# H3 convolution and feed-forward layer on one core: a larger descriptor room for GpSimd, `ones` read with a step of zero, the D skip added by a transfer

## The chip, the core and the metric

The kernel runs on one core of one Trainium2 chip. The metric is the time of one execution on the device in microseconds (us), as the median of several runs. The engines are TensorE (PE in the profile, its weight loads PEld), VectorE (DVE), ScalarE (ACT), GpSimd (POOL), and SyncE (SP), which here only issues transfers; 16 DMA engines carry out the transfers.

## What is computed

The reference, cut to what matters (S = 2048 positions, D = 1024 channels, F = 3584 hidden columns, all float32):

```python
xn = layernorm(A_q)
k_shift = causal depthwise convolution of A_k with A_shift_k   # 4 taps
kv = k_shift * A_v
y  = irfft(rfft(kv, 2*S) * rfft(A_ssm_k, 2*S))[:S]             # long causal convolution, per channel
y  = y + kv * A_ssm_D                                          # the D skip
out = A_q + xn * y + silu(xn @ B_w1) @ B_w2
```

The D skip is the same as adding `A_ssm_D` to the filter's first element, and that is how the kernel does it.

## The kernel before, in words

Two jobs share the core. The **feed-forward** job is matmuls in float16 with each operand split into a high and a low part, three matmuls for one product (lines 849 to 851 for the first matrix, 975 to 977 for the second). Its first matrix runs in plain units and then in units of seven products over pairs of columns (`units`); the second in plain form over 16 row tiles and two halves (`feed_forward`), and at the very end in eight units of seven products P1 to P7 (`units2`). Silu results go out to memory (`ht`) and come back as `wo` tiles, 13 of them in rotation. The weights of the second matrix are split by ACT and DVE into `x` tiles; those for `units2` are made while the plain form is still running, since they take over its places one by one.

The **convolution** job is done in eight groups of 128 channels. For each group SP loads the filter into `kf`; the D values are added to its first row; ACT takes the filter's squares for a scale (`hi<-kf`); `kv` is made in `acc` (DVE); PE transposes and transforms (`px`, `ps`); DVE does most of the transform and the product on `spec` and `tmp`; PE transforms back into `py`; and DVE multiplies by the normalized input `xg` into **`yt`**. A group has four `yt` tiles, and each goes out in two transfers of 128 KB that GpSimd issues and that **add** to the output in memory (helper `G`, line 279; `gated`, line 1589). `yt` has two places; a place comes free when both transfers of its tile have landed. The feed-forward results go out by the same helper (`out<-v`, `out<-hf`, `out<-w`, 256 KB each). GpSimd does little else, and issues them strictly in its program order. Before any of this the input is copied to the output by 16 plain transfers (`out<-in_x`).

The order of all instructions is fixed when the program is built: a planner (`Order.run`) holds a queue for each stream of work and always takes the head that can start first by its own price list, less a bias. A `G` has the price 1.1 us on GpSimd, and its data counts as landed 4.0 us later or when the planned transfer queue has come to it. Rings of tiles (`Ring`) say `ready()` when the uses of a place have been emitted in program order, not when they have happened. What the engines wait for on the chip are semaphores that follow from that order.

GpSimd writes descriptors of its transfers into a reserved stretch of on-chip memory; its size is `dynamic_dma_scratch_size`, 1024 bytes per partition. `ones`, a 128 x 128 tile of 512 bytes per partition, is read by PE in the warm-up and in the small sums of the scales (`norm`); `dr` is a tile of 512 bytes per partition for one group's D values.

Of the kernel before, what the change touches and what calls it, by code (L numbers as in the profile page):

```python
# [11 lines left out]
F32 = mybir.dt.float32  # L12
# [6 lines left out]
ADD, SUB, MUL = ALU.add, ALU.subtract, ALU.mult  # L19

P = 128
# [218 lines left out]
def h3_ffn_kernel(ctx, tc, x, kp, vs, fs, shift, dskip, w1, w2, cfwd, cinv, out):  # L240
    nc = tc.nc
# [3 lines left out]
    flag = defaultdict(Token)  # L245
# [12 lines left out]
    def size(a):  # L258
        n = 1
        for s in a.shape[1:]:  # L260
            n *= s
        return n

    def V(f, o, ins, us=None, m=0.15):
        return Op("DVE", us or 1.03 * (size(o) / 960 + 0.075), 0.16, f, ins, [o], m)
# [7 lines left out]
    def L(o, i, m=0.3):  # L273
        n = size(o) * o.shape[0] * mybir.dt.size(o.dtype)
        return Op("SP", 0.4, 0.1, lambda: nc.sync.dma_start(o, i), [i], [o], m, n)

    def G(o, i, m=0.3):
        n = size(i) * i.shape[0] * mybir.dt.size(i.dtype)
        return Op("POOL", 1.1, 4.0, lambda: nc.gpsimd.dma_start(o, i, accum_op=ADD), [i], [o], m, n)  # L279

    def v_tt(o, a, b, op, **k):
        return V(lambda: nc.vector.tensor_tensor(o, a, b, op=op), o, [a, b], **k)  # L282

    def v_stt(o, a, s, b, op0, op1, **k):
        return V(lambda: nc.vector.scalar_tensor_tensor(o, a, s, b, op0=op0, op1=op1), o,  # L285
                 [a, b] + ([] if isinstance(s, float) else [s]), **k)
# [31 lines left out]
    cst = ctx.enter_context(tc.tile_pool(name="cst", bufs=1))  # L318
# [10 lines left out]
    for n, e in enumerate((14 - 64, 10 - 64, 8 - 64, 64 - 23, 64)):  # L329
        nc.vector.memset(powers[:, n:n + 1], 2.0 ** e)  # L330
    invc = cst.tile([P, 1], F32, name="invc")
    ones = cst.tile([P, P], F32, name="ones")
    nc.vector.memset(ones, 1.0)
    ident = cst.tile([P, P], F32, name="ident")
    make_identity(nc, ident)
    taps = cst.tile([P, NG, TAPS], F32, name="taps")
# [12 lines left out]
    hts = Ring(order, wp, "ht", 4)  # L349
# [690 lines left out]
    def evacuate2(u, one, c, made, seen):  # L1040
# [3 lines left out]
        def copied(src, tok, to):  # L1044
            yield hfs.ready
            o, otok = hfs.tile([P, W])
            yield a_act(o, src, AF.Copy, invc2[:, 0:1])
            tok.set()
            yield G(to, o)
            otok.set()  # L1050
# [17 lines left out]
        yield v_stt(d, c[0], invc2[:, 0:1], d, MUL, ADD)  # L1068
        seen["P7"].set()
        yield G(at(u, 1, 1), d)  # L1070
        dt.set()
        if last:
# [9 lines left out]
        yield v_stt(a, c[0], invc2[:, 0:1], a, MUL, ADD)  # L1082
        c[1].set()
        yield L(at(u, 1, 0), a) if last else G(at(u, 1, 0), a)
        at_.set()

# [155 lines left out]
    def convolution(floor):  # L1242
# [5 lines left out]
        def ring(name, bufs, pool=ra):  # L1248
            return Ring(order, pool, name, bufs)

        kin_r, kf_r, dr_r, acc_r, hi_r, lo_r = (ring(*a) for a in (
            ("kin", 1), ("kf", 1), ("dr", 1), ("acc", 1), ("hi", 2), ("lo", 2)))
        tmp_r, csc_r, css_r = ring("tmp", 1), ring("csc", 2), ring("css", 2)
        ctxs["w2n"] = ring("w2n", 2)
        px_r, ps_r, py_r = ring("px", 1, ps_c), ring("ps", 2, ps_c), ring("py", 1, ps_c)
# [3 lines left out]
        more = {}  # L1259
# [14 lines left out]
        def loads():  # L1274
            for g in range(NG):
                for q in range(4):
                    b, ts = q // 2, q % 2 * TQ
                    yield kin_r.ready
                    kin, tok = kin_r.tile([P, 2 * TQ + HALO, P])
                    kt, kv = kin[:, 0:TQ + HALO], kin[:, TQ + HALO:]  # L1280
                    kins[g, q] = kt, kv, tok
                    yield L(kt, kp[g, b][:, ts:ts + TQ + HALO])
                    yield L(kv, vs[g, b][:, ts:ts + TQ])
                    flag["kin", g, q].set()
                    if q == 0:
                        yield kf_r.ready
                        kfs[g] = kf, _ = kf_r.tile([P, T2, 2, P], uses=4)
                        yield dr_r.ready
                        dr, dtok = dr_r.tile([1, P])
                        yield L(kf, fs[g])  # L1290
                        yield L(dr, dskip[g:g + 1, :])
                        yield v_tt(kf[0:1, 0, 0, :], kf[0:1, 0, 0, :], dr, ADD)
                        dtok.set()
                        flag["kf", g].set()

        def gate():
# [270 lines left out]
        def stage1_inv():  # L1567
            for g in range(NG):
                for t in TO:
                    yield flag["ipart", g, t]  # L1570
                    (hi, htok), (lo, ltok) = ipart.pop((g, t))
                    yield lambda: py_r.ready() or spare()
                    py, tok = (py_r if py_r.ready() else ff).tile([P, 2, 2, P])
                    for i in range(2):
                        def mm():
                            o = py[:, :, i, :]
                            ci = civ[:, t + 4 * i]
                            for c in range(2):
                                cs = slice(c * P, (c + 1) * P)
                                zs = slice(c * 2 * P, (c + 1) * 2 * P)  # L1580
                                nc.tensor.matmul(o, ci[:, 0, cs], hi[:, i, zs], start=(c == 0), stop=False)
                                nc.tensor.matmul(o, ci[:, 0, cs], lo[:, i, zs], start=False, stop=False)
                                nc.tensor.matmul(o, ci[:, 1, cs], hi[:, i, zs], start=False, stop=(c == 1))
                        yield T(mm, py[:, :, i, :], [hi[:, i], lo[:, i]], 0.66, m=1.0)
                    htok.set()
                    ltok.set()
                    add(gated(g, t, py, tok), CB)

        def gated(g, t, py, tok):
            yield flag["xg", g, t]  # L1590
            xg, xtok = xgs.pop((g, t))
            yield more["yt"].ready
            yt, ytok = more["yt"].tile([P, 2, 2, P], uses=2)
            sc, stok = scs[g]
            flat = [q.rearrange("p b i w -> p (b i w)") for q in (yt, py, xg)]
            yield v_stt(flat[0], flat[1], sc[:, 5:6], flat[2], MUL, MUL)
            tok.set()
            xtok.set()
            if t == TO[-1]:
                stok.set()  # L1600
            yield flag["copied"]
            for b in range(2):
                yield G(out4[b][:, :, t, g * P:(g + 1) * P], yt[:, b])
                ytok.set()
                flag["conv out"].set()

        for gen, bias in ((loads(), 0.05), (gate(), 0.04), (signal_parts(), CB), (stage1(), 0.02),
                          (transforms(), 0.02), (squares_w2(), 0.0), (rest(floor), 0.0)):
            add(gen, bias, floor)

    def change():

        yield flag["x done"]
        yield flag["spilled"]
        yield nm.ready
        early.close()
        convolution(max(order.free["DVE"], order.free["ACT"]))
# [95 lines left out]
```

## Time and profile before

| | |
|---|---|
| time, median of 3 runs | 1318.86 us (1317.51 to 1322.24) |
| the profiled execution's own time | 1314.44 us |
| its span | 1312.6 us, 1.84 us less than its own time |
| PE busy | 1255.1 us (96%) |
| DVE busy | 1166.1 us (89%) |
| ACT busy | 769.4 us (59%) |
| POOL busy | 126.3 us (10%), 127 adding transfers among it |
| software queue (GpSimd's transfers) | 24.91 MB, 14.6% of 16 engines' span |

Busy PE time is nearly the span, so the rest of the span is where PE had nothing to do: the start, some gaps, and the end. "Idle before, releaser" in a row says what an engine had waited for; "issue" as a releaser means that the profile shows no semaphore that it waited for.

### The profile page before, as it was taken

To read this page: it belongs to the slowest core of one execution; us is meant where nothing else is said; L and a number is where in the kernel's file an instruction comes from. 1 tells how busy PE (TensorE), PEld (TensorE's weight loads), DVE (VectorE), ACT (ScalarE), POOL (GpSimd) and SP (SyncE) were. 2 spreads that over 40 slices of the span, in tenths; PEclk is the share of its full clock that TensorE was granted. 3 is DMA by queue.
4 is the path that set the end of the run, shared out by engine and by line. 5 is a ranking of instruction groups with operands and counts; after the bars stand their busy time and mean duration, and the time that the engine had idled before them with its cause. 6 is when DMAs were issued, how large, how long until landed. Compare 5 with 4: busy or idle time off the path is not lost.

```text
span 1312.6 us, 17986 instructions
## 1 busy us (share of the span) xinstructions
PE 1255.1 (96%) x6146; PEld 610.2 (46%) x6146; DVE 1166.1 (89%) x1701; ACT 769.4 (59%) x1379; POOL 126.3 (10%) x133
## 2 busy tenths in 40 slices
PE   7899999899999989999999999999999999799993
PEld 6444544344444544445444544544544444344451
DVE  8999998999999679998999699699979979987981
ACT  6867987789566858878623622643442453535331
POOL 0000000000000011002100210210120020113222
PEclk8999999999999989999999999999999999899997
DMA  8456898899898789979975575687576478767855
GB/s 321 161 172 211 283 315 287 281 312 334 300 319 274 236 232 307 316 221 276 340 225 146 120 194 145 133 264 209 141 149 193 128 155 235 198 134 142 180 106 73
DMA packets 226012, 287.76 MB, mean 219 GB/s; under 512 B 16504, under 2 KB 135296, under 8 KB 223488
## 3 DMA queue, kind: packets, MB, share of 16 engines
q1 hardware_dynamic: 199440, 261.70, 61.2%
q0 software_dynamic: 26480, 24.91, 14.6%
q8 instruction: 48, 0.79, 0.3%
q14 instruction: 44, 0.36, 0.1%
HBM read 196.37 MB, written 98.57 MB: 225 GB/s over the span
## 4 chain that ended last, share of the span: by engine, by line
PE 43%; DVE 34%; issue 11%; DMA 7%; ACT 3%; POOL 2%; SPq 0%; POOLq 0%; DVEq 0%; ACTq 0%
DVE spec L282 10%; PE ff L851 7%; PE ff L849 7%; PE ff L850 7%; PE ff L976 6%; PE ff L977 6%; PE ff L975 5%; DVE tmp L282 5%; DVE ht L285 3%; DVE acc L285 3%; DVE x L285 2%; DMA out<-yt 2%; POOL out L279 2%; DVE spec L285 2%; DVE wo L285 1%
## 5 line engine op out<-in xcount | busy, mean ns | idle before, releaser
L976 PE MATMUL ff<-x,wo 128*128 128x512 f16 x864 | 328.4, 380 | 3.3 <-DVE x L285 3.3
L975 PE MATMUL ff<-x,wo 128*128 128x512 f16 x864 | 328.4, 380 | 1.5 <-ACT w L293 0.8
L977 PE MATMUL ff<-x,wo 128*128 128x512 f16 x864 | 328.4, 380 | 0.0
L849 PE MATMUL ff<-x,wo 128*128 128x512 f16 (+1 forms) x808 | 304.5, 377 | 7.3 <-DVE hf L282 3.2
L850 PE MATMUL ff<-x,wo 128*128 128x512 f16 (+1 forms) x808 | 304.5, 377 | 2.1 <-DVE x L285 2.1
L851 PE MATMUL ff<-x,wo 128*128 128x512 f16 (+1 forms) x808 | 304.3, 377 | 1.5 <-DVE wo L285 1.5
L282 DVE TENSOR_TENSOR spec<-spec 128x512 f32<-128x512 f32 (+2 forms) x256 | 261.7, 1050 | 1.7
L279 POOL DMA_DIRECT2D out<-yt x64 | 70.9, 1107 | 791.8 <-DMA wo<-ws 430.0
L977 PEld LDWEIGHTS <-wo 128*128 128x128 f16 x864 | 84.7, 98 | 106.8 <-issue 5.7
L975 PEld LDWEIGHTS <-wo 128*128 128x128 f16 x864 | 85.6, 99 | 97.5 <-issue 1.1
L976 PEld LDWEIGHTS <-wo 128*128 128x128 f16 x864 | 84.7, 98 | 99.4 <-issue 3.2
L851 PEld LDWEIGHTS <-wo 128*128 128x128 f16 x808 | 79.4, 98 | 98.5 <-issue 4.1
L850 PEld LDWEIGHTS <-wo 128*128 128x128 f16 x808 | 79.4, 98 | 96.6 <-issue 11.1
L849 PEld LDWEIGHTS <-wo 128*128 128x128 f16 x808 | 80.7, 100 | 86.9 <-issue 1.1
L282 DVE TENSOR_TENSOR tmp<-spec 128x2048 f32<-128x2048 f32 (+1 forms) x48 | 92.5, 1932 | 0.9
L285 DVE SCALAR_TENSOR_TENSOR ht<-hf,wsc,ht 128x512 f16<-128x512 f32 x104 | 76.4, 744 | 6.6 <-ACT ht L293 6.5
L293 ACT ACTIVATE ht<-hf,wsc 128x512 f16<-128x512 f32 x104 | 74.6, 719 | 6.8 <-DVE hf L282 4.5
L285 DVE SCALAR_TENSOR_TENSOR acc<-kin,taps,acc 128x512 f32<-128x512 f32 x96 | 71.4, 743 | 2.5 <-ACT acc L293 2.4
L293 ACT ACTIVATE wo<-raw,wsc 128x512 f16<-128x512 f32 x84 | 59.3, 711 | 15.0 <-DVE raw L282 15.0
L279 POOL DMA_DIRECT2D out<-v x39 | 36.7, 940 | 308.1 <-ACT v L293 274.8
L293 ACT ACTIVATE spec<-spec 128x1024 bf16<-128x1024 f32 x32 | 33.7, 1055 | 55.3 <-DVE spec L282 55.2
L285 DVE SCALAR_TENSOR_TENSOR wo<-raw,wsc,wo 128x512 f16<-128x512 f32 x84 | 61.9, 742 | 3.4 <-ACT wo L293 3.2
(192 smaller groups left out, 1820.3 us busy)
## 6 DMA issues: line engine op xcount, KB each, us to landing
wo<-hs SPq DMA_DIRECT2D x160, 256.0 KB, 3.7
w2n<-in_w SPq DMA_DIRECT2D x91, 256.0 KB, 4.6
ws<-wo SPq DMA_DIRECT2D x84, 256.0 KB, 3.5
wo<-ws SPq DMA_DIRECT2D x84, 256.0 KB, 4.6
hs<-ht SPq DMA_DIRECT2D x80, 256.0 KB, 3.5
raw<-in_w SPq DMA_DIRECT2D x28, 512.0 KB, 5.5
kin<-in_kp SPq DMA_DIRECT2D x32, 448.0 KB, 3.5
out<-v POOLq DMA_DIRECT2D x39, 256.0 KB, 4.5
```

The source lines that it names most:

```text
L279: return Op("POOL", 1.1, 4.0, lambda: nc.gpsimd.dma_start(o, i, accum_op=ADD), [i], [o], m, n)
L282: return V(lambda: nc.vector.tensor_tensor(o, a, b, op=op), o, [a, b], **k)
L285: return V(lambda: nc.vector.scalar_tensor_tensor(o, a, s, b, op0=op0, op1=op1), o, [a, b] + ([] if isinstance(s, float) else [s]), **k)
L293: nc.scalar.activation(o, i, func, scale=scale, **kw)
L849: nc.tensor.matmul(o, w[:, 0, k], xf[:, :, k, 0], start=first and k == 0, stop=False, **kw)
L850: nc.tensor.matmul(o, w[:, 0, k], xf[:, :, k, 1], start=False, stop=False, **kw)
L851: nc.tensor.matmul(o, w[:, 1, k], xf[:, :, k, 0], start=False, stop=last and k == KH - 1, **kw)
L975: nc.tensor.matmul(po, hx[:, n, 0, :], wc[:, n, 0, :], start=first and n == 0, stop=False, **kw)
L976: nc.tensor.matmul(po, hx[:, n, 0, :], wc[:, n, 1, :], start=False, stop=False, **kw)
L977: nc.tensor.matmul(po, hx[:, n, 1, :], wc[:, n, 0, :], start=False, stop=last and n == 3, **kw)
```

## The change

Five edits. The descriptors' room is doubled, from 1024 to 2048 bytes per partition. `ones` shrinks to one column that is read 128 times with a step of zero. The tile `dr`, its load by SP and the DVE addition of the D values go; in their place GpSimd issues a transfer of 512 bytes that adds the D values to `kf` directly. `yt` may take a place of the ring `hts` (the silu results) once the first matrix is done, if its own two are not ready. And the planner's price of a `G` falls from 4.0 to 3.0 us after the issue.

```diff
     def G(o, i, m=0.3):
-        return Op("POOL", 1.1, 4.0, lambda: nc.gpsimd.dma_start(o, i, accum_op=ADD), [i], [o], m, n)
+        return Op("POOL", 1.1, 3.0, lambda: nc.gpsimd.dma_start(o, i, accum_op=ADD), [i], [o], m, n)
...
-    ones = cst.tile([P, P], F32, name="ones")
-    nc.vector.memset(ones, 1.0)
+    one = cst.tile([P, 1], F32, name="one")
+    nc.vector.memset(one, 1.0)
+    ones = one.to_broadcast([P, P])
...
-                        yield dr_r.ready
-                        dr, dtok = dr_r.tile([1, P])
                         yield L(kf, fs[g])
-                        yield L(dr, dskip[g:g + 1, :])
-                        yield v_tt(kf[0:1, 0, 0, :], kf[0:1, 0, 0, :], dr, ADD)
-                        dtok.set()
+                        yield G(kf[0:1, 0, 0, :], dskip[g:g + 1, :])
...
-            yield more["yt"].ready
-            yt, ytok = more["yt"].tile([P, 2, 2, P], uses=2)
+            r = more["yt"]
+            yield lambda: r.ready() or flag["gemm1"]() and hts.ready()
+            yt, ytok = (r if r.ready() else hts).tile([P, 2, 2, P], uses=2)
...
-    nc = bacc.Bacc("TRN2", target_bir_lowering=False, num_devices=1, dynamic_dma_scratch_size=1024)
+    nc = bacc.Bacc("TRN2", target_bir_lowering=False, num_devices=1, dynamic_dma_scratch_size=2048)
```

Since the planner sets the order, it moves too, from the first group's filter on. GpSimd at the end of the program, before: `yt0` and `yt1` are the two places of `yt`, `x2` is the two halves of one tile, and `hf`, `w` and `v` are results of the last unit of the feed-forward job.

```order
L279 DMA out_0<-hf0_11807 128x512
L279 DMA out_0<-yt0_11832 256x1x128 x2
L279 DMA out_0<-v0_11692 128x512
L279 DMA out_0<-yt1_11875 256x1x128 x2
L279 DMA out_0<-yt0_11912 256x1x128 x2
L279 DMA out_0<-yt1_11946 256x1x128 x2
L279 DMA out_0<-hf1_11954 128x512
L279 DMA out_0<-w_11955 128x512
L279 DMA out_0<-hf0_12002 128x512
```

GpSimd at the same place now:

```order
L279 DMA out_0<-yt0_11792 256x1x128 x2
L279 DMA out_0<-yt1_11830 256x1x128
L279 DMA out_0<-hf1_11834 128x512
L279 DMA out_0<-yt1_11830 256x1x128
L279 DMA out_0<-yt0_11868 256x1x128
L279 DMA out_0<-v0_11689 128x512
L279 DMA out_0<-yt0_11868 256x1x128
L279 DMA out_0<-yt1_11911 256x1x128 x2
L279 DMA out_0<-hf2_11940 128x512
L279 DMA out_0<-w_11941 128x512
L279 DMA out_0<-hf1_11986 128x512
```

Four tiles and the last three results stand there as before; the other results stand between the halves of tiles. On PE the last `py` product has 63 feed-forward matmuls behind it, where it had 42.

GpSimd at the fifth group's `yt` tiles, before (group five's filter needs nothing of GpSimd there):

```order
L279 DMA out_0<-v0_9103 128x512
L279 DMA out_0<-yt0_9176 256x1x128 x2
L279 DMA out_0<-yt1_9206 256x1x128 x2
L279 DMA out_0<-yt0_9260 256x1x128 x2
L279 DMA out_0<-yt1_9302 256x1x128 x2
L279 DMA out_0<-v1_9368 128x512
```

And now, where a filter's D values (`kf<-in_dskip`) are issued ahead of the tiles:

```order
L279 DMA kf_8924<-in_dskip 1x16x8
L279 DMA out_0<-v0_9005 128x512
L279 DMA out_0<-yt0_9116 256x1x128 x2
L279 DMA out_0<-yt1_9146 256x1x128 x2
L279 DMA out_0<-yt0_9200 256x1x128 x2
L279 DMA out_0<-yt1_9242 256x1x128 x2
L279 DMA out_0<-v1_9259 128x512
```

Two places of `yt` in turn, as before: all 32 tiles of the program take `yt0` and `yt1` in turn, and none takes a place of `hts`.

ACT at the first group's filter, before (`hi<-kf` are the squares, `wo` and `ht` are high parts of the feed-forward job, `ff2<-ff3` frees one of its accumulators):

```order
L293 ACTIVATE wo9_2464<-t1_2357,wsc_181 128x512
L293 ACTIVATE hi0_2470,css0_2346<-kf_2361 128x1024
L293 ACTIVATE ff2_2488<-ff3_2404 128x512
L293 ACTIVATE wo10_2493<-raw3_2139,wsc_181 128x512
L293 ACTIVATE hi1_2476,css0_2346<-kf_2361 128x1024
L293 ACTIVATE hf2_2452<-hf2_2452,wsc_181 128x512
```

And now:

```order
L293 ACTIVATE wo9_2459<-t1_2357,wsc_181 128x512
L293 ACTIVATE ht1_2398<-x4_958,wsc_181 128x4x128
L293 ACTIVATE ff2_2484<-ff3_2403 128x512
L293 ACTIVATE wo10_2491<-raw3_2139,wsc_181 128x512
L293 ACTIVATE ht2_2405<-x4_958,wsc_181 128x4x128
L293 ACTIVATE hf2_2451<-hf2_2451,wsc_181 128x512
L293 ACTIVATE ht3_2509<-hf1_2416,wsc_181 128x4x128
L293 ACTIVATE wo11_2514<-raw3_2139,wsc_181 128x512
L293 ACTIVATE hi0_2467,css0_2346<-kf_2361 128x1024
L293 ACTIVATE v1_2486<-ff2_2484 128x512
```

The squares have moved seven places back, behind feed-forward work.

## Rows read from the trace of the kernel before

**Rows 1.** The page, part 1: busy time and share of the span.
```profile
PE 1255.1 (96%) x6146; PEld 610.2 (46%) x6146; DVE 1166.1 (89%) x1701; ACT 769.4 (59%) x1379; POOL 126.3 (10%) x133
```

**Rows 2.** Busy time of each engine by stretch; last columns granted clock, DMA share, GB/s.
```profile
478.90:482.90 4.00, 0.45 (x3) 0.05 (x2) 0.85 (x2) 0.99 (x2) 0.68 (x1) 0.88 0.33 77
...
1126.90:1143.20 16.30, 9.06 (x41) 3.91 (x40) 16.27 (x23) 10.36 (x17) 2.02 (x3) 0.92 0.79 209
1139.00:1147.70 8.70, 6.77 (x20) 2.60 (x21) 8.28 (x14) 4.76 (x8) 0.12 (x1) 0.61 0.25 55
...
1295.80:1312.60 16.80, 0.00 (x0) 0.00 (x0) 0.66 (x1) 0.00 (x0) 4.87 (x5) 0.56 0.61 86
...
1303.00:1306.00 3.00, 0.00 (x0) 0.00 (x0) 0.00 (x0) 0.00 (x0) 1.51 (x3) 0.50 1.03 123
```

**Rows 3.** POOL in order of time, third convolution group: start, us, instruction [idle before <-releaser].
```profile
725.37 1.10 POOL L279 DMA_DIRECT2D out<-yt  x1 [7.66 <-DVE yt L285]
729.79 1.11 POOL L279 DMA_DIRECT2D out<-yt  x1 [3.32 <-issue]
...
754.07 1.10 POOL L279 DMA_DIRECT2D out<-yt  x1 [2.82 <-issue]
754.65 1.45 POOL L279 DMA_DIRECT2D out<-v  x1
```

**Rows 4.** Transfers: count, KB, median us to landing; adding transfers after 1265, min/median/max.
```profile
wo<-hs SPq DMA_DIRECT2D x160, 256.0 KB, 3.7
...
out<-yt POOLq DMA_DIRECT2D x64, 128.0 KB, 3.9
...
DMA to landing us min/median/max: 3.1/4.0/6.6
```

**Rows 5.** What DVE waited for from 715 to 1070: us in total, times, longest.
```profile
DVE yt L285 <- ACT xg L293: 12.5, 2, 6.3
DVE yt L285 <- PE ps L1391: 11.2, 4, 2.8
DVE yt L285 <- DMA out<-yt: 11.1, 2, 5.7
```

**Rows 6.** All engines in order of time, the end of the program.
```profile
1283.40 0.75 DVE L285 SCALAR_TENSOR_TENSOR yt<-py,csc,xg 128x512 f32<-128x512 f32 x1 [7.01 <-DMA out<-yt]
...
1296.49 0.34 SPq L275 DMA_DIRECT2D out<-v  x1
...
1305.57 1.22 POOL L279 DMA_DIRECT2D out<-hf  x1
...
1284.20 0.27 PE L1581 MATMUL py<-zh,civ 128*128 128x256 f16 x1 [2.12 <-DVE yt L285]
```

**Rows 7.** DVE and PE in order of time, in the first unit of `units2`.
```profile
1142.02 2.07 DVE L285 SCALAR_TENSOR_TENSOR x<-x,tau,x 128x512 f16<-128x512 f32 x3
...
1146.61 0.63 PE L976 MATMUL ff<-x,wo 128*128 128x512 f16 x1
1147.04 0.63 PE L977 MATMUL ff<-x,wo 128*128 128x512 f16 x1
...
1148.37 0.38 PE L976 MATMUL ff<-x,wo 128*128 128x512 f16 x1
1148.59 0.38 PE L977 MATMUL ff<-x,wo 128*128 128x512 f16 x1
```

**Rows 8.** DVE and ACT in order of time at the first and fourth filter.
```profile
215.75 0.28 DVE L282 TENSOR_TENSOR kf<-kf,dr 1x128 f32<-1x128 f32 x1 [1.35 <-DMA kf<-in_fs]
...
216.06 1.06 ACT L293 ACTIVATE hi<-kf 128x1024 bf16<-128x1024 f32 x1 [1.32 <-DMA ws<-wo]
...
618.69 0.27 DVE L282 TENSOR_TENSOR kf<-kf,dr 1x128 f32<-1x128 f32 x1
...
626.67 1.04 ACT L293 ACTIVATE hi<-kf 128x1024 bf16<-128x1024 f32 x1
```

**Rows 9.** PE in order of time at the start: the warm-up.
```profile
1.20 6.54 PE L1648 MATMUL ft<-ones 128*128 128x128 f32 x44 [1.20 <-DVE ones L333]
```

More of the change, by code (lines that the diff above doesn't have):

```diff
@@ L1249, in ring @@
             return Ring(order, pool, name, bufs)
-        kin_r, kf_r, dr_r, acc_r, hi_r, lo_r = (ring(*a) for a in (
-            ("kin", 1), ("kf", 1), ("dr", 1), ("acc", 1), ("hi", 2), ("lo", 2)))
+        kin_r, kf_r, acc_r, hi_r, lo_r = (ring(*a) for a in (
+            ("kin", 1), ("kf", 1), ("acc", 1), ("hi", 2), ("lo", 2)))
         tmp_r, csc_r, css_r = ring("tmp", 1), ring("csc", 2), ring("css", 2)
```

## The prediction

> **What bounds the kernel now.** I read the busy shares first. PE is busy for 1255.1 of 1312.6 us [rows 1], so a change that adds or removes no matmuls can only gain what PE loses in gaps, at a lower clock, and after its last matmul. Next I read the stretches. After 1295.8 us PE does nothing more, yet the span runs 16.8 us on with POOL at work [rows 2]; that is the largest loss that one cause may explain. From 1126.9 to 1143.2 PE is busy 9.06 of 16.30 us, while DVE is busy 16.27: here DVE is late. From 478.9 to 482.9 PE loses another 3.55 us.
>
> Then POOL in order of time, in a convolution group. The second `yt` transfer starts 4.42 us after the first, and POOL sat idle 3.32 us "for issue", with no semaphore to wait for. A result transfer behind a `yt` transfer, however, starts only 0.58 us after it [rows 3]. The median `yt` transfer lands 3.9 us after its issue [rows 4]. My reading: the room for descriptors holds one `yt` transfer and one result, and not two `yt` transfers, so each `yt` waits until the one before it has landed. The code gives the sizes behind this: a `yt` transfer consists of 256 rows of 512 bytes, a result of 128 rows of 2 KB. If one `yt` and one result fit in the old room, two of each fit in the new one.
>
> That slow pace holds the two `yt` places, and DVE stands before `yt`: in the four groups between 715 and 1070 us it waited 12.5 + 11.2 + 11.1 us ahead of `yt` [rows 5], some 8.7 us in a group. The releasers named there are various, since ACT and PE had long been done in some of them; the place was what came last.
>
> **The change, part by part.** I sum against the profiled execution, 1314.44 us with a span of 1312.6; it is 4.4 us below the median of the runs, and I carry the difference over to the median.
>
> *The end, -9.9 us.* Before, the last result transfer is issued at 1305.57 and the span ends 7.0 us later [rows 6]. It was ready long before: PE's last matmul ended at 1295.67. With room for three transfers or more the eight `yt` transfers of the last group go out as DVE makes them, and the order helps: the last `py` has 63 matmuls behind it instead of 42, at 0.22 us 13.6 us. Then nothing is queued when PE ends. What is left: SP's store of the last tile starts 0.8 us after PE's end (1296.49), lands 3.5 to 4.5 us later (a `wo` load of the same size 3.7, adding transfers 3.1 to 6.6 [rows 4]), and the closing takes some 1.8 us (7.0 less 5.2 of landing, which I put between the median and the longest of [rows 4]). That is 6.1 to 9.2 us, I take 7.0: 16.9 - 7.0 = 9.9, with ends at 7.7 and 10.8.
>
> *The last group's wait, -2.1 us.* DVE waited 7.01 us for a `yt` place, and PE 2.12 us for that DVE row [rows 6]. It goes with the pace; at worst nothing of it goes.
>
> *The gap before `units2`, -8.3 us.* The gap is 16.30 - 9.06 = 7.24 us. In its last part the granted clock over 8.7 us is 0.61, so part of this stretch is at 1.2 instead of 2.4 GHz: eleven matmuls follow at a pitch of 0.43 instead of 0.22 us [rows 2, 7], 2.3 us more. DVE has no idle time there [rows 2] while it makes the last weights of `units2`, from 1142.02 on [rows 7]; it is simply late, and its last idle time before was in the sixth group, ahead of the third and fourth `yt` (2.8 and up to 5.7 us [rows 5]). With the new room, the third `yt` can start when the first tile's two transfers have landed: issue some 1.2 us after DVE's row begins, 1.1 us for the second, 4.0 of landing, so 6.3 us; before it was 1.2 + 4.42 + 3.9 = 9.5. The fourth's place comes free some 3 us after the third's, with two more issues, where the old pace made it wait 5.7 to 6.3 us more [rows 5]. Of the 8.5 us of both waits I take 6, since ACT still has to normalize the fourth's input. So DVE leaves the sixth group 6 us earlier. Does the new order eat this? Between the last `yt` of that group and the last weights it holds 83 us of DVE work instead of 77.5 (its rows by the mean durations), 5.4 more, and PE passes 360 matmuls to the same point instead of 330, 6.5 us more. That is a wash, 1.1 us to the good. I take 6.0 of the 7.24 us, and the whole 2.3, since pieces that stay short should not cost clock. Ends: 0 and 9.5.
>
> In the groups before, PE has next to no gaps, so DVE's 6 us there buy nothing by themselves.
>
> *The gap at 479, no change.* PE waits there for a `yt` whose place is held by a transfer that waits for the last copies of the input. Their place on SP is the same. The later transfers now share the engines with it: 0 to 0.5 us worse.
>
> *The D skip, +1.0 us.* Eight DVE rows of 0.28 us go [rows 8]; DVE is not the bound in most places, so I count nothing. Eight POOL issues come, at 1.1 us each like `yt` [rows 3], each ahead of `yt` or result transfers that then wait behind it for the filter's load. POOL has over 7 us idle ahead of a group [rows 3]. The data lands 1.1 + 3.1 to 6.6 us after the filter, where DVE took 0.28. From the third group on the squares come 8 us or more after the filter (the tightest is the fourth: 618.69, then 626.67 [rows 8]), which covers it. In the first they follow at once (215.75, then 216.06 on ACT [rows 8]); the order has put them seven ACT rows back, at 0.7 us 4.9 us, about what the transfer takes. If ACT is held, its silu rows and high parts are queued behind, and PE waits for those. So 0 to 3 us for the first two groups, and I take 1.0, for the order covers most of it. The Trainium skill, "DMA: Bandwidth & Descriptors", section "Anatomy of one DMA — SWDGE (gpsimd) path", gives such a transfer a fixed cost of about 2.0 us plus its bytes over 436 GB/s; by that the estimate for 512 bytes is 2.0 us and this term would be nil. It gives 2.3 us for a `yt` transfer, where the row has 3.9, so the trace does not bear it out for adding transfers.
>
> *`ones` with a step of zero, 0.* The warm-up ends at 7.74 us [rows 9], and PE then waits for DVE anyway. *`yt` in places of `hts`: 0,* since no tile goes there: `ready()` looks at what has been emitted, and by then the own place always counts as free. *The lower price of a `G`* acts through the order alone, counted above.
>
> Sum: -9.9 - 2.1 - 8.3 + 1.0 = -19.3 us, 1314.4 to 1295.1 for a profiled execution, and 1318.9 to 1299.6 for the median.
>
> **The rivals.** *Only the end gains.* DVE's factors are late all the same, because the planner, believing in cheaper transfers, has put them 5.4 us further back, or another gap of that size opens where the order moved (between 205 and 260 us, say). For it: PE's gaps there come from where DVE's rows stand, and such an order is touchy. Against: the sum above. Time: -9.9 - 2.1 + 1.0 = -11.0, 1308 us.
>
> *The room does not set the pace.* If adding transfers to memory are taken one at a time, or the room that counts is another, the pace stays at 3.7 us. For it: the spacing is just the time to landing. Against: the 0.58 us behind a `yt`. Then the end gains only the earlier `py`, 21 matmuls at 0.22, 4.5 us, the factors cost 5.4, the D skip 1.0: 1321 us, no difference.
>
> *Slower: the bursts starve PE.* Close to the end, three transfers keep all 16 engines busy (1.03) at 123 GB/s [rows 2]. Eight `yt` transfers, 1 MB, now in one burst, would hold them 8.5 us, and PE's `wo` loads, one per 2.6 us, queue beside them. The Trainium skill, "DMA: Bandwidth & Descriptors", section "Issuing engines are not separate DMA queues", says that transfers of all engines interleave on the same 16; that share agrees, and it speaks against buying speed with more in flight. The price: if the lead of the loads is below 8.5 us, each burst stalls PE by some 3.5 us and costs 2.5 us of clock, six bursts 36 us, less the gain 1318.9 + 36 - 19 = 1336 us. Against: 13 places at 2.6 us allow a lead of 33 us, and a load lands in 3.7 us [rows 4].
>
> **How the numbers follow.** The forecast, 1299.6 us, has 0.62, with its terms' bounds from 1290 to 1306; only the end gains, 0.23; the room does not set the pace, 0.09; slower by the bursts or in another way 0.06. The predicted time is 1299.6. The range from 1290 to 1310 takes in the first rival. About 0.5%, 6.6 us, is what a measurement of this kernel can tell from no change; faster than 1312.3 are the first two cases, so 0.85; the third case is the same, 0.10 with some of the last; slower 0.05.
>
> **What would show it.** In the changed profile the two halves of a `yt` tile start about 1.1 us apart with no idle time for issue; DVE's wait ahead of the third and fourth `yt` of a group falls from 8.7 to some 3 us; PE's gap between 1120 and 1150 is below 2 us, with a granted clock of 1.00; the span ends 7 us after PE's last matmul. If halves are still 3.7 us apart, the room was not it. If the gap before `units2` is still there, the order ate the 6 us. If PE waits for `wo` loads, the bursts collide. A longer warm-up than 6.54 us, or ACT idle ahead of the squares of the first filter for more than 3 us, would make small terms wrong. The prediction is most at risk from gaps at places that the new order opens, which no row of before shows.

## The result, and the profile after

The changed kernel takes 1296.5 us (median of 4 runs, 1296.0 to 1297.6) where the kernel before, measured beside it, takes 1318.2 (1316.1 to 1322.2): a ratio of 0.983, with a 95% interval from 0.981 to 0.986. The forecast was 1299.6 us with a range from 1290 to 1310. The medians are 21.7 us apart, the two profiled executions 17.7 in their spans, since the kernel before was profiled in an execution quicker than its four timed ones.

| profiled execution | before | after | change |
|---|---|---|---|
| span, us | 1312.6 | 1294.9 | -17.7 |
| PE's last matmul ends at | 1295.7 | 1290.6 | -5.1 |
| tail behind it | 16.9 | 4.3 | -12.6 |
| PE busy | 1255.1 | 1256.0 | +0.9 |
| PE idle before its end | 40.6 | 34.6 | -6.0 |

Part 1 of the page of the changed kernel, to be held against [rows 1]:

```profile
PE 1256.0 (97%) x6146; PEld 611.8 (47%) x6146; DVE 1164.3 (90%) x1693; ACT 769.5 (59%) x1379; POOL 132.7 (10%) x141
```

No engine's work has changed by more than 2 us, except POOL's, which grew by 6.4; the time came out of waiting. Two thirds of it came out of the tail. POOL in order of time, in the third convolution group and in the last, after (columns as in [rows 3]):

```profile
722.70 2.25 POOL L279 DMA_DIRECT2D out<-yt  x2 [7.62 <-DVE yt L285]
725.77 1.08 POOL L279 DMA_DIRECT2D out<-yt  x1 [0.82 <-DVE yt L285]
727.39 1.11 POOL L279 DMA_DIRECT2D out<-yt  x1 [0.53 <-issue]
...
1278.87 2.21 POOL L279 DMA_DIRECT2D out<-yt  x2 [0.77 <-DVE yt L285]
...
1289.11 0.89 POOL L279 DMA_DIRECT2D out<-hf  x1 [1.90 <-ACT hf L293]
```

Both halves of the first tile stand in one row ("x2"), 2.2 us for the two, where [rows 3] had 4.42 us from one start to the next. Those of the tile behind it start 1.62 us apart. In the last group the `yt` tiles are out at 1281, and POOL waits for ACT's last results instead of being late with them. All of the program's idle time of POOL that the trace puts down to "issue" has fallen from 165.2 to 2.8 us. The end, in order of time (PE and SP):

```profile
1290.22 0.38 PE L978 MATMUL ff<-x,wo 128*128 128x512 f16 x1
...
1291.41 0.34 SPq L275 DMA_DIRECT2D out<-v  x1
```

SP's store is the last thing that leaves, 0.8 us behind PE, and 3.5 us later the span ends. In [rows 6] POOL's last transfer left 9.1 us after that store.

Now the places where the forecast wanted the rest. Windows of the changed kernel (columns as in [rows 2]: busy time of PE, PEld, DVE, ACT, POOL, then clock, DMA share, GB/s):

```profile
240.00:275.00 35.00, 28.55 (x121) 12.26 (x119) 31.31 (x54) 26.09 (x46) 0.00 (x0) 0.90 0.86 272
725.00:1075.00 350.00, 349.60 (x1735) 170.53 (x1734) 314.58 (x383) 151.53 (x277) 55.65 (x56) 1.00 0.70 172
1126.90:1143.20 16.30, 10.16 (x37) 3.80 (x35) 15.65 (x23) 6.62 (x11) 1.75 (x2) 0.77 0.63 157
```

The first two windows for the kernel before:

```profile
240.00:275.00 35.00, 31.36 (x142) 14.21 (x141) 33.07 (x61) 29.56 (x53) 0.00 (x0) 0.95 0.89 289
725.00:1075.00 350.00, 345.77 (x1711) 167.49 (x1710) 306.36 (x377) 151.86 (x276) 51.38 (x51) 1.00 0.66 166
```

In the four groups between 725 and 1075 us PE lost 4.2 us in small gaps and now loses 0.4. The gap before `units2` is still there: 6.1 us idle where [rows 2] has 7.2, and a lower clock than before. And between 240 and 275 us PE now loses 6.5 us, where it lost 3.6. PE's own rows at these two places, after:

```profile
248.83 0.58 PE L850 MATMUL ff<-x,wo 128*128 128x512 f16 x1 [3.17 <-DVE hf L282]
259.01 0.59 PE L850 MATMUL ff<-x,wo 128*128 128x512 f16 x1 [3.28 <-DVE hf L282]
...
1134.11 0.38 PE L977 MATMUL ff<-x,wo 128*128 128x512 f16 x1 [2.16 <-DVE x L285]
1136.98 0.59 PE L977 MATMUL ff<-x,wo 128*128 128x512 f16 x1 [2.06 <-DVE x L285]
```

What DVE waited for from 715 to 1070 us (total, times, longest), to be held against [rows 5]:

```profile
DVE spec L282 <- ACT spec L293: 14.5, 8, 3.8
DVE yt L285 <- ACT xg L293: 9.1, 8, 1.5
...
DVE yt L285 <- PE py L1580: 2.3, 4, 0.6
```

The wait ahead of `yt` has gone from 34.8 to 9.1 us, 8.7 to 2.3 in a group, as forecast (with the short waits for `py`, 1.5 us before, it is 36.3 to 11.4). But a wait that was not there has come up behind it: 14.5 us for ACT's `spec` rows. At the sixth group's last `yt` one sees how (DVE):

```profile
1051.79 0.75 DVE L285 SCALAR_TENSOR_TENSOR yt<-ff,csc,xg 128x512 f32<-128x512 f32 x1 [1.50 <-ACT xg L293]
1055.44 0.69 DVE L282 TENSOR_TENSOR spec<-spec,ps 128x512 f32<-128x512 f32 x1 [2.90 <-ACT spec L293]
```

and ACT in the same 4 us:

```profile
1052.13 1.05 ACT L293 ACTIVATE hi<-kf 128x1024 bf16<-128x1024 f32 x1
...
1053.17 1.05 ACT L293 ACTIVATE hi<-kf 128x1024 bf16<-128x1024 f32 x1
...
1054.21 0.71 ACT L293 ACTIVATE acc<-kin,taps 128x512 f32<-128x512 f32 x1
1054.83 1.07 ACT L293 ACTIVATE spec<-ps 128x512 f32<-128x512 f32 x2
```

DVE wants the copy of a product (`spec<-ps`), which stands on ACT behind the next filter's squares and a tap. As I read it, ACT had time for all of that while DVE stood before `yt` for 5 us, and now it hasn't. DVE's idle time from 725 to 1075 us has fallen by only 8.2 us (43.6 to 35.4), some 2.5 in a group of about 106 us, where the forecast took 6.0.

### The profile page after: what moved, and what is told of

Its sections match the earlier page's. It is cut to its first block, busy times and chain, and to the rows that moved or that the text cites. A ratio compares the mean times of both kernels' runs of the same rounds, so it can differ in the third digit from the quotient of the medians.

```text
span 1294.9 us, 17972 instructions
## 1 busy us (share of the span) xinstructions
PE 1256.0 (97%) x6146; PEld 611.8 (47%) x6146; DVE 1164.3 (90%) x1693; ACT 769.5 (59%) x1379; POOL 132.7 (10%) x141
## 4 chain that ended last, share of the span: by engine, by line
PE 69%; DVE 19%; DMA 6%; ACT 3%; issue 3%; SPq 0%; DVEq 0%; ACTq 0%
PE ff L977 11%; PE ff L978 11%; PE ff L976 11%; PE ff L850 9%; PE ff L852 9%; PE ff L851 9%; DVE spec L282 4%; DVE x L285 2%; DVE tmp L282 2%; DMA w2n<-in_w 2%; DVE ht L285 2%; PE ps L1386 2%; PE ps L1388 2%; PE ps L1387 2%; DVE wo L285 1%
## 5 line engine op out<-in xcount | busy, mean ns | idle before, releaser
L293 ACT ACTIVATE v<-ff,invc 128x512 f32<-128x512 f32 x40 | 27.4, 686 | 91.4 <-PE ff L978 76.6
```

Source lines behind the costliest of these rows:

```text
L293: nc.scalar.activation(o, i, func, scale=scale, **kw)
```

## The experiments

Each time stands beside runs of the kernel before on the same chip. Its medians lie 5 us apart (1313.2 to 1318.2), so ratios are compared. Where the last column says "one run" there is no interval.

| run | room | D skip | differs also in | us | ratio to before, 95% |
|---|---|---|---|---|---|
| changed kernel | 2048 | transfer | | 1296.5 | 0.983 (0.981 to 0.986) |
| e1_old_room | 1024 | transfer | | 1323.5 | 1.007 (1.005 to 1.010) |
| e2_price4 | 2048 | transfer | price 4.0 | 1296.3 | 0.986 (0.983 to 0.989) |
| e3_old_room_price4 | 1024 | transfer | price 4.0 | 1323.2 | 1.007 (1.006 to 1.009) |
| e4_room1536 | 1536 | transfer | | 1295.9 | 0.986 (0.984 to 0.988) |
| e5_dve_dskip | 1536 | DVE | | 1289.5 | 0.981 (0.979 to 0.983) |
| e6_no_dskip | 2048 | left out | | 1295.1 | 0.985 (0.983 to 0.988) |
| e8_full_ones | 1536 | transfer | full `ones` | 1294.9 | one run |
| e10_small_edits | 1024 | DVE | | 1315.6 | 1.000 (0.998 to 1.001) |
| e11_room1280 | 1280 | DVE | | 1290.9 | one run |
| e9_factors_first | 1536 | DVE | factors earlier | 1288.7 | 0.979 (0.976 to 0.982) |
| e12_factors_a_little | 1792 | DVE | factors a little earlier | 1284.7 | 0.976 (0.974 to 0.978) |
| e13_factors_room1792 | 1792 | DVE | factors earlier | 1286.8 | 0.978 (0.975 to 0.980) |

**The room undone, the rest kept.**

```diff
-    nc = bacc.Bacc("TRN2", ..., dynamic_dma_scratch_size=2048)
+    nc = bacc.Bacc("TRN2", ..., dynamic_dma_scratch_size=1024)
```

> The changed kernel with the old room (1024) and nothing else different: the instructions stand in the same order on every engine. Theory (the room sets the pace of the `yt` transfers): halves of a `yt` tile are 3.7 us apart again with some 2.5 us of idle time for issue between them, DVE waits for a `yt` place again in the last groups, PE ends at some 1294 us instead of 1290.6, and the tail after PE's last matmul is some 13 us (16.9 of the kernel before, less the 4 us by which the last `py` comes earlier). Time 1312 to 1322 us. Rival (the new order alone brings the gain, the room is only used when it is there): within 3 us of the changed kernel, 1294 to 1300.

1323.5 us, 2.2 to 2.4% above the changed kernel by the ratios and slower than the kernel before. POOL in its second-last group, in order of time:

```profile
1199.51 1.10 POOL L279 DMA_DIRECT2D out<-yt  x1 [2.48 <-issue]
1203.04 1.09 POOL L279 DMA_DIRECT2D out<-yt  x1 [2.42 <-issue]
1206.61 1.10 POOL L279 DMA_DIRECT2D out<-yt  x1 [2.48 <-issue]
```

3.5 us from one half to the next, with the idle time for issue back in each row, 153.0 us in all. The trace also has the landing of each transfer. In this run 53 `yt` transfers stand right behind another `yt` transfer; none starts before that one has landed, and 51 start 0.26 to 0.38 us after. In the kernel before it is the same (0.26 to 0.33 us). In the changed kernel 49 of the 53 start before the landing. The tail is 13.3 us, and PE ends at 1311.2 us, where I had expected some 1294: in this order the room is worth more through PE's waits than through the tail. The order of the rows is that of the changed kernel, so these 2.2 to 2.4% are the room's alone. That the rest of the change costs 0.7% was not expected; it is followed up below.

**The planner's price put back.**

```diff
-        return Op("POOL", 1.1, 3.0, ...
+        return Op("POOL", 1.1, 4.0, ...
```

> The changed kernel with the planner's old price of an adding transfer (4.0 instead of 3.0), the room kept at 2048: only the order differs. Theory (the room brings the gain, the order is worth a few us either way): 1295 to 1303 us; halves of a `yt` tile back to back; the last `py` again has some 42 matmuls behind it, so the tail after PE's last matmul grows from 4.3 to 6 to 9 us. If the gap before `units2` (6.1 us idle in 1125 to 1150) stands because the new order puts DVE's factors 5.4 us later, it shrinks here to 0 to 2 us and gives back 4 to 6 us. Rival (the order is what gained): 1308 to 1318.

> Old room and old price: the kernel before with the cheap `ones`, the D skip as a transfer and the free choice of a place for `yt`. Theory: 1318 to 1321 us, the D skip costing 0 to 3 us and the other two edits nothing; tail 16 to 18 us. Rival (the small edits carry part of the gain, DVE having eight rows less): 1312 to 1316.

With 3.0 and with 4.0 every row of every engine stands in the same place: the price edit has no effect, and the two runs repeat the changed kernel and the run before. They show how far equal programs differ: 0.983 and 0.986, 1.007 and 1.007. It also shows that the planner's shift of DVE's rows, which the prediction laid to cheaper transfers, is the D skip's. Both runs missed what I expected of the tail (the last `py` did not move back) and of the old room (10 us slower than before, not 0 to 3).

**How much room it takes.**

> The changed kernel with a room of 1536, half way. Theory: if the old room holds one `yt` transfer (256 rows) and one result (128 rows) but not two `yt` transfers, this room holds two `yt` transfers at least, and the halves of one tile go back to back, while the next tile waits when it comes within 4 us. Time 1296 to 1303 us, idle time for issue on POOL only behind pairs. Rival (a room must hold more for the next transfer to start, or the pace goes by another measure): halves 2.5 to 4 us apart, time 1308 to 1320.

> The same with a room of 1280. If room is counted in rows and 1024 holds one `yt` transfer of 256 rows and one result of 128 but not two `yt` transfers, 1024 holds 384 to 511 rows, and 1280 holds 480 to 639: two `yt` transfers fit in the upper part of that. If they fit, halves start 1.1 us apart and the time is 1288 to 1296 us; if not, 3.7 us apart and 1310 to 1318 us.

Half of the added room brings the whole gain, and in a single run a quarter brings nearly all of it (PE ends at 1281.0 us, but the tail is 8.1 us, where it is 4.9 with 1536). The second of these runs, and the one with 1536 beside it, have the D skip on DVE. POOL's idle time for issue falls on, though:

| room | 1024 | 1280 | 1536 | 1792 | 2048 |
|---|---|---|---|---|---|
| run | e10 | e11 | e5 | e12 | changed kernel |
| issue, us in all | 164.8 | 34.2 | 32.2 | 5.8 | 2.8 |

(The last two have other orders of rows; in the order of the changed kernel a room of 1536 has 28.4.) With 1280 two `yt` transfers fit, but the third still waits: in the last group transfers start 1.5 to 2.1 us apart. Whether the room is counted in rows or in bytes was not tried.

```profile
1274.04 1.10 POOL L279 DMA_DIRECT2D out<-yt  x1 [1.00 <-issue]
1275.64 1.10 POOL L279 DMA_DIRECT2D out<-yt  x1 [0.50 <-issue]
1277.49 1.11 POOL L279 DMA_DIRECT2D out<-yt  x1 [0.75 <-issue]
```

**The D skip back on DVE, in a room of 1536 and of 1024.** The first has the room and the two small edits (`ones`, the places of `hts`) in the order of the kernel before; the second has the small edits alone. Both keep the new price of a `G`, which moves no row here either.

```diff
-                        yield G(kf[0:1, 0, 0, :], dskip[g:g + 1, :])
+                        yield L(dr, dskip[g:g + 1, :])
+                        yield v_tt(kf[0:1, 0, 0, :], kf[0:1, 0, 0, :], dr, ADD)
+                        dtok.set()
```

> The changed kernel with the D skip back on DVE (its tile and its load from SP with it) and a room of 1536, which leaves the memory for that tile and was as good as 2048 in the run before. Every engine's rows then stand in the order of the kernel before (the warm-up's operand apart), so this is the room alone. Theory (the D skip's transfer costs some 10 us, since the old room with the small edits was 9.9 us slower than the kernel before): 1284 to 1291 us; one PE gap of some 3.2 us at 254 instead of two at 249 and 259, and less than 2 us of PE idle time from 1120 to 1150. Rival (the D skip costs about the 1.0 us of the prediction with the new room, and cost 10 only where POOL was blocked): 1294 to 1298 us.

> The run with the D skip on DVE, but in the old room of 1024: what is left of the change is the step of zero in `ones` and the free choice of a place for `yt`; every engine's order is that of the kernel before. Theory (these two cost and bring nothing, the room is all): within 4 us of the kernel before, halves of a `yt` tile 3.7 us or more apart, a tail of 16 to 18 us. Rival (one of the two edits is worth something): 5 us or more off the kernel before.

The small edits alone change nothing (1.000, 0.998 to 1.001). Room alone takes 1.9% off, more than the whole change does. This pair differs in nothing but the room, and every row stands in the same order, so one can compare stretches between the same two rows of PE: around 480 us, where the first `yt` tiles go out; from the third group to a matmul ahead of the gap before `units2`; and from there to one behind that gap. The small edits alone, in the old room:

```profile
462.82:515.33 52.51, 46.53 (x201) 20.81 (x200) 42.46 (x53) 32.91 (x68) 7.71 (x7) 0.90 0.91 254
...
725.15:1110.48 385.33, 380.49 (x1873) 183.18 (x1871) 341.24 (x417) 162.21 (x294) 55.35 (x55) 1.00 0.67 172
1110.48:1164.80 54.32, 47.91 (x210) 21.90 (x209) 52.34 (x78) 24.67 (x41) 6.92 (x8) 0.91 0.67 172
```

The same stretches with the room of 1536:

```profile
464.46:509.26 44.80, 42.06 (x201) 19.52 (x200) 40.23 (x51) 31.88 (x67) 7.71 (x7) 1.00 1.00 293
...
721.27:1099.30 378.03, 378.03 (x1872) 183.92 (x1870) 343.95 (x419) 163.89 (x295) 55.28 (x55) 1.00 0.69 176
1099.30:1151.65 52.35, 46.35 (x211) 21.38 (x210) 50.99 (x76) 24.56 (x41) 6.92 (x8) 0.93 0.69 174
```

In the groups PE takes 7.3 us less, 4.8 of them gaps. Around the gap before `units2` it takes 2.0 us less, but of its 6.4 us of idle time only 0.4 goes. The tail goes from 15.2 to 4.9 us. Around 480 us 7.7 us go; there the kernel before, in the old room too, takes 49.0 us for the same rows, so 3.5 us of this vary from one execution to the next. The last group gives 4.1 us.

I had expected less than 2 us of idle time before `units2`, so that expectation fell, and with it the prediction's own reserve, that a new order might eat DVE's time: no new order is at work here. Half of that idle time is one row, the same in both (PE in order of time, the old room first):

```profile
1140.42 1.12 PE L1356 MATMUL px<-ident,acc 128*128 128x128 f32 x4 [3.24 <-DVE ht L285]
...
1127.50 0.66 PE L1356 MATMUL px<-ident,acc 128*128 128x128 f32 x4 [3.24 <-DVE ht L285]
```

The kernel before has the same 3.24 us there. This is PE's wait for DVE's `ht` rows of the next convolution group, and the room did not change it.

**The D skip left out, the order kept.**

```diff
-                        yield G(kf[0:1, 0, 0, :], dskip[g:g + 1, :])
+                        op = G(kf[0:1, 0, 0, :], dskip[g:g + 1, :])
+                        op.emit = lambda: None
+                        yield op
```

> The changed kernel, its order untouched on every engine, with the eight D skip transfers not issued (the output lacks the D skip). Theory A (the cost lies in the order that the planner makes around a D skip that it believes to land late): nothing is gained, 1293 to 1298 us, the PE gaps at 249 and 259 stay. Theory B (the cost is the transfer itself, POOL's issue and the wait for its landing): 1284 to 1291 us, and the gaps at 249 and 259 shrink to one of 3 us.

1295.1 us and 0.985: the eight transfers cost nothing that can be measured. What costs is the order that the planner makes for a D skip that it takes to land late. PE's two gaps stay without any transfer (PE in order of time):

```profile
246.72 0.59 PE L850 MATMUL ff<-x,wo 128*128 128x512 f16 x1 [3.21 <-DVE hf L282]
257.16 0.58 PE L850 MATMUL ff<-x,wo 128*128 128x512 f16 x1 [3.28 <-DVE hf L282]
```

With the D skip on DVE (the run with 1536) there is one:

```profile
254.18 0.38 PE L850 MATMUL ff<-x,wo 128*128 128x512 f16 x1 [3.24 <-DVE hf L282]
```

In the old room the same order and its transfers cost 0.7%. One wait there looks like the transfer's own: the second half of a `yt` tile stands on POOL beside a D skip, and the profile names the filter's load as its releaser (POOL in order of time, changed kernel in the old room, and the landing of the first of these transfers):

```profile
606.01 1.09 POOL L279 DMA_DIRECT2D out<-yt  x1 [6.38 <-DVE x L285]
615.64 1.10 POOL L279 DMA_DIRECT2D out<-yt  x1 [8.54 <-DMA kf<-in_fs]
616.22 1.36 POOL L279 DMA_DIRECT2D kf<-in_dskip  x1
...
DMA to landing us min/median/max: 9.3/9.3/9.3
```

But the first half landed 9.3 us after its start, at 615.3, and the second starts 0.31 us later, as the others do in this room. So this wait is the room's too. What makes up the 0.7% was not found.

**The full `ones`.**

> The changed kernel with the full tile of ones for the warm-up, in a room of 1536; nothing else differs. If the step of zero makes the warm-up's matmuls slower, the 44 take 6.5 us again (7.5 in the changed kernel, 6.9 to 7.9 in four others with the step of zero); if the clock does it, 6.5 to 7.9. The time stays at 1293 to 1299 us either way, since PE waits for DVE behind the warm-up.

The warm-up's 44 matmuls take 7.63 us with the full tile, and 6.62 to 7.86 in the runs with the step of zero. The step costs nothing; the 6.54 of [rows 9] is one end of a spread.

**The factors of `units2` earlier.** If the gap before `units2` comes from the amount of DVE's work between the sixth group's `yt` and the last factors, it closes when the factors are made earlier, in the groups, where PE now has no gaps.

```diff
-  add(split(... tau[:, j // 2:j // 2 + 1], ...), 0.05)
-  add(split(... tau2[:, i:i + 1], toks), 0.05)
-  (norms_w2(), 0.03)
+  add(split(... tau[:, j // 2:j // 2 + 1], ...), 0.03)
+  add(split(... tau2[:, i:i + 1], toks), 0.4)
+  (norms_w2(), 0.4)
```

> Room 1536, D skip on DVE, and the planner prefers the rows that make the factors of `units2` (three weights in the planner: 0.05 and 0.03 become 0.4, another 0.05 becomes 0.03). Theory (the gap before `units2` stands because DVE has too much to do between the sixth group's `yt` tiles and the last factors, whatever comes before it; factors made earlier, in the groups where PE has no gaps, close it): PE idle from 1110 to 1150 falls from 5.9 to below 2 us, with a clock of 1.00, and the kernel takes 1281 to 1287 us instead of 1289.5. Rival (DVE is bound all through the second half, so rows moved ahead make others late): the gap opens elsewhere between 600 and 1100 us, and the time is 1288 to 1300 us.

The window around the gap (columns as above):

```profile
1110.00:1150.00 40.00, 38.73 (x191) 18.91 (x190) 39.66 (x55) 20.53 (x34) 6.05 (x7) 1.00 0.77 191
```

The gap is closed: 1.3 us idle instead of 6.0, the clock at 1.00, and PE ends 8.1 us earlier, at 1274.5. The time is 0.2% better only, inside the interval and above the 1281 to 1287 us that I had expected: the tail is 12.5 us. The last `py` has 12 matmuls behind it, so the last `yt` tiles come when PE is nearly done. POOL in order of time, at the end of this run:

```profile
1272.59 0.88 POOL L279 DMA_DIRECT2D out<-w  x1 [4.24 <-issue]
1273.22 2.50 POOL L279 DMA_DIRECT2D out<-yt  x2
1278.92 2.20 POOL L279 DMA_DIRECT2D out<-yt  x2 [3.20 <-issue]
1280.23 1.81 POOL L279 DMA_DIRECT2D out<-hf  x1
```

Two more runs ask whether this is the room or the order: the same with a room of 1792, and a weaker preference (0.1 for the two raised weights, the third left as it was) in that room.

> The strong preference again, with a room of 1792 instead of 1536 and nothing else changed. If the tail of 12.5 us there came from the room (POOL stood idle 4.2 and 3.2 us for issue among the last transfers), it shrinks to 7 to 9 us here and the kernel takes 1283 to 1286 us. If it came from the order alone (the last `py` 12 matmuls from the end), the tail stays at 11 to 13 us and the time at 1287 to 1290 us.

> D skip on DVE, a room of 1792, and the planner's preference for the factors of `units2` raised less than in the run before (0.05 and 0.03 become 0.1). The last `py` product has 27 matmuls behind it, where it had 12 with the strong preference and 42 without any. Theory (what the strong preference gained before `units2` it lost at the end, since the last `py` and so the last `yt` transfers came late): PE idle from 1110 to 1150 is some 3 to 4 us, PE ends at 1277 to 1280, the tail is 5 to 8 us, time 1283 to 1288 us. Rival (DVE is bound in the second half and any preference only shifts the loss): 1288 to 1292 us.

With 1792 the strong preference keeps a tail of 11.8 us: the order made it, for the most part. (POOL still sits idle 4.8 us for issue ahead of the same `w`; a larger room in this order was not tried.) The weak one leaves 2.8 us of PE's idle time before `units2`, has a tail of 6.7 us, and takes 1284.7 us, 0.976 (0.974 to 0.978). That is the fastest kernel of this study, 2.4% below the kernel before and 0.7 to 1.0% below the changed one by the ratios.

## Why the prediction was right, step by step

**Right in its reading of the cause.** "The room for descriptors holds one `yt` transfer and one result, and not two `yt` transfers" is what the runs show: with 1024 the halves are 3.5 us apart, with 1280 and more they are not, and nothing else of the change moves the time down. All that the prediction named as proof came (halves 1.1 us apart, the wait ahead of `yt` at some 3 us or less) except the gap before `units2` and its clock; the end came closer behind PE than the 7 us that it named.

**The end, -9.9 us, was -12.6.** The mechanism held. What was mis-sized is the rest behind PE: forecast 7.0 us (0.8 to the store, some 4.4 of landing, 1.8 of closing), measured 4.3. The trace has the landings: the store's takes 2.6 us and the closing behind it 0.9. In the kernel before the last result's landing took 5.7 us, where I had put 5.2, and the closing 1.4.

**The last group's wait, -2.1 us, came.** PE's 2.12 us before the last but one `py` product is gone. DVE's waits for a `yt` place did not end (3.90 us at 1277.7, 7.01 before); PE no longer stands behind them.

**The gap before `units2`, -8.3 us, was -1.1.** This is the step that failed. Its first half was right: DVE's wait ahead of `yt` fell by 6.4 us in a group. The step from there, "so DVE leaves the sixth group 6 us earlier", was not, and three things in the runs tell why. First, behind the last `yt` stands a row that needs ACT, and DVE now waits there. Of two waits in a row the first was removed, and the next one took more than half of it. (That ACT's squares make this wait is how the rows read; no run took them away.) I had named the question for the row itself ("ACT still has to normalize the fourth's input") and left it out for the row behind. Second, what counts at the gap is DVE's lead over PE, and PE came earlier too. In the pair with the same order DVE's idle time in the stretch from the third group on falls by 10.0 us; PE's time for that stretch falls by 7.3, and DVE has done only 2.7 us more work at its end. Third, I took the whole gap as DVE's lateness with the last weights; with the order of before, 3.24 us of it are the wait of `px`, which did not move. The prediction would have let the new order take the blame; the pair with the same order shows the same gap, so it is not that. The runs with the factors earlier show what does close it: less DVE work between the group and `units2`.

The 2.3 us of clock did not come back either: from 1126.9 to 1143.2 us the granted clock is 0.77. In the run with the weak preference, where 2.8 us of idle time are left, it is 1.00 from 1110 to 1150.

**The groups' small gaps, counted as nothing, were -3.8.** "PE has next to no gaps, so DVE's 6 us there buy nothing": 4.2 us in 350 are few, but as large as other terms of the sum. In the pair with the same order the stretch gives 7.3 us.

**The D skip, +1.0 us with a bound of 3, was +5 to 6** (1289.5 with DVE's, 1295.1 with the changed order, on one chip). Each part that I priced (issue, landing, ACT's wait) is nil: ACT waits 0.2 us for a D skip. Not priced was that the planner plans around it. I saw the squares seven places back on ACT and read it as cover. It is part of an order that costs: between 240 and 275 us PE loses 2.8 us more, and its clock there falls from 0.95 to 0.90. Which row of that order makes PE wait was not tried. The first rival had named this place ("between 205 and 260 us, say"), and a gap came there; the late factors, which it laid to the new order too, stood with the old order as well.

**The small ones.** `ones` 0 and `hts` 0, as forecast: together 1.000 (0.998 to 1.001). The price of a `G`, "through the order alone", moved no row. The gap at 479 was forecast at 0 to 0.5 us more; it went from 3.55 to 4.12. No burst starved PE: a `wo` load lands in 3.4 us, 3.7 before.

The sum was made against the profiled execution, and there 17.7 of the 19.3 us came. The median came out below its forecast because the kernel before was profiled in an execution 4.4 us below its median. So the forecast of 1299.6 held although the gap and the D skip came out 7.2 and some 4.5 us worse; the end and the groups came out 2.7 and 3.8 us better, and smaller shares elsewhere did the rest. It was right on the cause and on the end, and lucky in the sum.

## What to carry to other kernels

Idle time "for issue" ahead of GpSimd's transfers, ending when the one before has landed, was here the sign of a descriptor room that is too small; try the next sizes up and stop at the first that removes the pace. When a wait is removed, look at the row behind it on the same engine, and ask which engine had only kept up because of that wait. Where two kernels have the same rows in the same order, compare stretches between the same rows, not between the same microseconds. In a kernel whose order a planner makes, an edit costs what it does to the plan: hold the order still and leave the work out, and the two costs come apart.

## What was new about the hardware

The time that an adding transfer took to land differed more between two stretches of the program than between two sizes. The medians of the changed kernel are 4.3 us for the D skip's 0.5 KB and 4.6 for `yt`'s 128 KB, but they mix two stretches. Landings of the D skip (four transfers) and then of `yt`, from 215 to 625 us, where the DMA engines were busy for 0.91 of the time:

```profile
DMA to landing us min/median/max: 4.8/5.4/6.1
DMA to landing us min/median/max: 4.4/6.9/8.2
```

The same from 700 to 1040 us, where the share was 0.68:

```profile
DMA to landing us min/median/max: 2.0/2.8/3.7
DMA to landing us min/median/max: 3.3/4.4/6.1
```

The rule that the prediction cited (the Trainium skill, "DMA: Bandwidth & Descriptors", section "Anatomy of one DMA — SWDGE (gpsimd) path") gives an estimate of 2.0 us for the small one and 2.3 for `yt`. The quickest small one took that 2.0; no `yt` came below 3.1 in any of these runs. The second surprise is how sharp the step is: from 1024 to 1280 the kernel with the order of before gains 25 us (1315.6 to 1290.9, the latter in one run), and next to nothing more with 1536 (1289.5).
